# Seven quarter products for the second matrix product of eight late expert tiles, and a planner with new costs and free choice of buffers

## The chip, the cores and the metric

The kernel runs on one core of a Trainium2 chip. The metric is device time in microseconds of one execution; lower is better. All data are 32-bit floats.

## What is computed

A spectral mixing block feeds a mixture of experts.

```
X = rfft(x, axis=1); Y = X * (filt_r + i filt_i); y = irfft(Y)     x: 8 x 2496 x 256
t = y.reshape(19968, 256)
logits = t @ w_gate                                                 8 experts
e = argmax(logits); g = softmax(logits)[e]
out = g * (relu(t @ w1[e]) @ w2[e])                                 w1: 256 x 1024, w2: 1024 x 256
```

## The kernel before

**Two kinds of work.** The transform runs batch by batch in four stages of matrix products, a to d (`stage_a`, L498, to `stage_d`, L548), since 2496 = 39 x 64. Between stages the data are stored to device memory and loaded in another layout (`zd`, `ud`), except in the first batch, which stays on chip. After stage d the logits are taken, every row is given a place in the list of its expert (`route`, L707), and GpSimd scatters the rows there by indirect DMA (`scatter`, L825).

The expert work goes by tiles of rows of one expert. There are 65 in the plan: 28 of 512 rows (tiles 1 and 7 to 33), 14 of 256 rows and 23 of 128 (the last two run only if needed). `TILES`, `SHORT` and `PLACE` (L900 to 906) name them; `PLACE` is tile 34, the first 256-row tile after the last of 512 rows, and `SHORT` is 42. `rows_in` (L912) loads a tile's rows, four transfers and one for the gate values, `turn_x` (L954) transposes them on VectorE, `weights` (L933) loads a half of `w1` or `w2`, 512 KB each. The first product of the large tiles is made by seven quarter products of width 256 (`hidden_by_quarters`, L979, with sums of the weights by GpSimd in `w1_sums`, L969). The second product is made plainly (`result`, L1042): for each 128 rows eight accumulating matmuls of width 256, one instruction that scales by the gate value, one indirect DMA to the output. Until the transform has ended, and for tiles up to `PLACE`, `w2` comes in two halves per tile; from then on all of `w2` lies on chip in `w2s`, which is loaded bit by bit beside the last large tiles.

**What sets the order.** The program is straight-line code; no engine chooses. While it is built, `Order` (L125) keeps a clock for each engine and for the transfers; `count` (L177) adds an estimated time for every instruction that is issued. The main loop (L1323 to 1360) takes a transform step or a piece of expert work whose inputs are ready by these clocks: `first_products` (L1222) and `second_products` (L1259) are two streams of such pieces. `more_loads` (L1143) issues transform loads while fewer than seven input buffers are held, `prefetch` (L1186) issues rows and weights when `rows_at` (L810) says that the rows have landed. `Slots` (L243) records the buffers of a pool; a new tile takes the oldest buffer of its name in turn. PSUM has seven banks under the name `bank` (L367). SyncE issues nearly all plain DMAs, in program order, so a load waits behind whatever was issued ahead of it; GpSimd issues the indirect ones.

Nearly every instruction is recorded at L238, the line of the issuing helper, so groups are told apart by tile names: `fin` are transform inputs, `xT` the transposed rows, `hT` the hidden values, `w1t`, `w2t` the halves of the weights, `wsum` and `sums` the sums for the quarters.

Of the kernel before, what the change touches and what calls it, by code (L numbers as in the profile page):

```python
# [19 lines left out]
P = 128  # L20
# [104 lines left out]
class Order:  # L125
# [5 lines left out]
    def __init__(self, nc):  # L131
        self.nc = nc
        self.t = dict.fromkeys(("tensor", "vector", "scalar", "gpsimd", "sync", "transfers"), 0.0)
        self.slow = self.busy = self.last = 0.0
        self.done, self.used, self.slots, self.ahead = {}, {}, {}, {}
        self.tensor, self.vector, self.scalar, self.gpsimd, self.sync = (
            Issue(self, name) for name in ("tensor", "vector", "scalar", "gpsimd", "sync"))
# [33 lines left out]
    def transfer(self, out, in_):  # L171
        n = min(self.run(out), self.run(in_), 4096)
        packet = float(np.interp(n, (32, 64, 256, 1024, 4096), (9, 11, 18, 46, 159)))
        size = 4 * int(np.prod([d[1] for d in in_.ap]))
        return size / n * packet / 14e3

    def count(self, engine, op, args, named):  # L177
        aps = [a for a in list(args) + list(named.values()) if isinstance(a, bass.AP)]
        if not aps:
            return  # L180
        out, ins = aps[0], aps[1:]
        if "out" in named:
            out = named["out"]
            ins = [a for a in aps if a is not out]
        if op.endswith("value_load"):
            out, ins = None, aps
        at = named.get("out_offset")
        if at is not None:
            ins.append(at.ap)
        kept = [a for a in ins if a.space != DRAM or a.name[:2] in ("zd", "ud")]  # L190
        free = self.t[engine]
        start = max([free] + [self.ready(a) + (self.HOP if engine != "sync" else 0.0) for a in kept])
        if out is not None:
            start = max(start, self.ahead.pop(out.name, 0.0))
            n = int(np.prod([d[1] for d in out.ap][1:])) if out.space != DRAM else 0
        tail = 0.0
        if op.endswith("dma_start"):
            busy = 1.3 if engine == "gpsimd" else 0.4
            self.t[engine] = start + busy
            took = self.transfer(out, named["in_"])  # L200
            self.t["transfers"] = max(self.t["transfers"], start + busy) + took
            end, tail = self.t["transfers"], self.LOAD
        else:
            if out is None:
                took = 0.02
            elif engine == "tensor":
# [35 lines left out]

class Slots:  # L243
    def __init__(self, order, pool, bufs):
        self.order, self.pool, self.bufs, self.tiles, self.n = order, pool, bufs, {}, {}

    def free(self, tag, k=0):

        past, n = self.tiles.get(tag, []), self.n.get(tag, 0)
        if len(past) + k < n or k >= n:  # L250
            return 0.0
        name = past[k - n]
        return max(self.order.done.get(name, 0.0), self.order.used.get(name, 0.0)) + 0.1

    def tile(self, shape, dtype, **named):
        new = self.pool.tile(shape, dtype, **named)
        past = self.tiles.setdefault(named.get("tag") or named.get("name"), [])
        n = self.n[named.get("tag") or named.get("name")] = named.get("bufs") or self.bufs
        if len(past) >= n:
            name = past[-n]  # L260
            self.order.ahead[new.name] = max(self.order.done.get(name, 0.0), self.order.used.get(name, 0.0)) + 0.1
        past.append(new.name)
        return new


# [1 line left out]
def kernel(  # L267
# [86 lines left out]
    vld = cst.tile([P, 2 * NG + 2], F32, name="vld")  # L354


    first = ExitStack()
# [94 lines left out]
    ins, outs, lgs, yts, lands = {}, {}, {}, {}, []  # L452
    NIN, YB = 7, 6

    moves, stored = [], set()

# [250 lines left out]
    def route(b, c0, c1):  # L707
# [196 lines left out]
    SHORT = next(i for i in range(NT) if TILES[i][0] == 1)  # L904

    PLACE = next(i for i in range(NT) if TILES[i] == (2, B - 1))
    late = {}

    def quarters(i):
# [23 lines left out]
    def weights(h, second):  # L933
# [10 lines left out]
            return  # L944
        ev = nc.sync.value_load(work[i][1], min_val=0, max_val=E - 1)
        if second:
            w2t[h] = pools["moe"].tile([P, FH2, D], F32, tag="w2t", name="w2t", bufs=2)
            nc.sync.dma_start(out=w2t[h], in_=moe_w2[bass.ds(ev, 1), k].rearrange("o p i d -> p (o i) d"))
        else:
            pool, bufs = (late["w1"], 8) if i >= SHORT else (pools["moe"], 3)  # L950
            w1t[h] = pool.tile([P, DH, 2, 2 * P], F32, tag="w1t", name="w1t", bufs=bufs)
            nc.sync.dma_start(out=w1t[h], in_=moe_w1[bass.ds(ev, 1), k].rearrange("o p i h f -> p (o i) h f"))
# [89 lines left out]
    def result(i, j):  # L1042
# [5 lines left out]
        p = bank()  # L1048
        for k in range(FT):
            w2 = late["w2s"][:, bass.ds(ev, 1), k, :] if i >= PLACE else w2t[2 * i + k // FH2][:, k % FH2, :]  # L1050
            mm(p[:, :D], lhsT=hs[i][k % 4 // 2][:, k // 4, k % 2, j * P:(j + 1) * P], rhs=w2, start=(k == 0), stop=(k == FT - 1))
        ys = pools["moe"].tile([P, D], F32, tag="ys", name="ys", bufs=4)
        gate = gis[i][:, j, 8:9]
        either(p, D, lambda: nc.vector.tensor_scalar(ys, in0=p[:, :D], scalar1=gate, scalar2=None, op0=ALU.mult),
               lambda: nc.scalar.activation(ys, p[:, :D], AF.Copy, scale=gate))
        nc.gpsimd.indirect_dma_start(
            out=out,
            out_offset=bass.IndirectOffsetOnAxis(ap=gis[i].bitcast(U32)[:, j, :1], axis=0),
# [4 lines left out]
        )  # L1063


    sides = []

    def count(kind):
# [74 lines left out]
    def more_loads():  # L1143
# [4 lines left out]
            kind, at = {"z": ("a", zd), "u": ("c", ud)}[key[0]]  # L1148
            return (kind, key[1]) in stored and nc.ready(at[key[1]]) <= max(t["tensor"], t["sync"]) + 0.5

        while todo and len(ins) < NIN and (len(lands) < NIN or lands[-NIN] not in ins):
            n = 0
            if not stored_for(todo[0]):

# [7 lines left out]
            lands.append((kind, b, c))  # L1162

    def after(b):
        for rows, n in GROUPS[b]:
# [20 lines left out]
    def prefetch():  # L1186
# [6 lines left out]
        for what in ("w1", "w2"):  # L1193
            h = got[what]
            if h < 2 * min(len(work), NT - RARE) and rows_at[work[h // 2][3]] <= t["tensor"] and (
                    h - used[what] < ((3 if h < 2 * SHORT else 8) if what == "w1" else 2 if h < 2 * PLACE else 8)):
                weights(h, what == "w2")
                asked.add((what, h))
                got[what] += 1
        for h in range(used["w1"], got["w1"]):  # L1200
            if quarters(h // 2) and h not in wsum and len(wsum) < 2 and nc.ready(w1t[h]) <= max(t["tensor"], t["gpsimd"]) + 0.3:
                w1_sums(h)

    def when(key):

# [2 lines left out]
        if what == "w2":  # L1208
            if halves[0] <= n or key not in asked:
                return None  # L1210
            return max(ps.free("bank"), nc.ready(*hs[i], *((late["w2s"],) if i >= PLACE else (w2t[2 * i], w2t[2 * i + 1]))))
        if key not in asked or what != "x" and n % 2 and ends[0] < i:
            return None
        if what == "x":
# [44 lines left out]
    def second_products():  # L1259

        for i in range(NT - RARE):
            for j in range(TILES[i][0]):
                yield lambda: result(i, j), 3.42, ("w2", 2 * i + 1)
            hs.pop(i), gis.pop(i), w2t.pop(2 * i, None), w2t.pop(2 * i + 1, None)
            used["w2"] += 2
            ends[0] += 1

    def rare_tiles():

# [17 lines left out]
    with tc.manual_schedule(engines=None):  # L1287
# [35 lines left out]
        while fs or any(heads):  # L1323
# [27 lines left out]
            if not fs and not sides and not late:  # L1351
                fft.close()
                tail = late["tail"] = open_pool(ctx, name="tail", bufs=1)
                late["w1"] = open_pool(ctx, name="w1b", bufs=8)
                late["n"] = 0
                late["pads"] = pad_rows()
                late["w2s"] = tail.tile([P, E, FT, D], F32, name="w2s")
            prefetch()
            if used["x"] > SHORT and "need" not in late:
                late["need"] = nc.values_load(need, min_val=0, max_val=GROUPS[-1][-1][1])  # L1360
# [32 lines left out]
```

## Time and profile before

| What | Value |
|---|---|
| runs, us | 1499.45, 1493.14, 1496.27 (median 1496.27) |
| profiled execution, us | 1494.36, span 1492.7 |
| mean granted TensorE clock | 0.991 |
| TensorE busy | 1451.7 us, 7396 records |
| VectorE, ScalarE, GpSimd busy | 770.7, 471.8, 733.4 us |
| matmuls with `w2t` | 1984 records, 447.5 us busy |
| matmuls with `w2s` | 592 records, 132.6 us busy |
| VectorE adds of `hT` from a bank | 128x512: 686 ns; 128x256: 421 ns |
| GpSimd sums | 128x256: 742 ns; 128x512: 1270 ns |
| indirect DMA to the output | 161, 998 ns of GpSimd each |

A plain f32 matmul of the program is two records in the profile. The page gives busy time, count and mean length of one record for each group; records of TensorE overlap, so busy time is less than count times mean length, and the time that one takes is best read from the distance of starts in the timeline. "Idle before" is the time in which the engine stood still ahead of a group, with what ended it.

### The profile page before, as it was taken

To read this page: it belongs to the slowest core of one execution; us is meant where nothing else is said; L and a number is where in the kernel's file an instruction comes from. 1 tells how busy PE (TensorE), PEld (TensorE's weight loads), DVE (VectorE), ACT (ScalarE), POOL (GpSimd) and SP (SyncE) were. 2 spreads that over 40 slices of the span, in tenths; PEclk is the share of its full clock that TensorE was granted. 3 is DMA by queue.
4 is the path that set the end of the run, shared out by engine and by line. 5 is a ranking of instruction groups with operands and counts; after the bars stand their busy time and mean duration, and the time that the engine had idled before them with its cause. 6 is when DMAs were issued, how large, how long until landed. Compare 5 with 4: busy or idle time off the path is not lost. (4 is left out here: it accounts for less than half of the span.)

```text
span 1492.7 us, 24448 instructions
## 1 busy us (share of the span) xinstructions
PE 1451.7 (97%) x7396; PEld 1148.8 (77%) x7396; DVE 770.7 (52%) x1732; ACT 471.8 (32%) x983; POOL 733.4 (49%) x1053
## 2 busy tenths in 40 slices
PE   8898997999989999999999999999999999999998
PEld 6553555776667777777787888887888889999997
DVE  4667677354577656565764555537344334441110
ACT  4453442333322233222233222222222222223332
POOL 3434455344446656554555756764546455741111
PEclk9999999999999999999999999999999999999999
DMA  9749889678767756474456545545455543456661
GB/s 255 252 152 333 289 306 295 207 258 280 251 182 229 219 157 169 131 239 128 128 152 196 130 117 149 147 139 145 151 178 176 167 146 106 117 187 179 181 179 52
DMA packets 216376, 278.10 MB, mean 186 GB/s; under 512 B 124131, under 2 KB 163708, under 8 KB 216245
## 3 DMA queue, kind: packets, MB, share of 16 engines
q1 hardware_dynamic: 197125, 233.19, 52.7%
q0 software_dynamic: 19120, 43.33, 8.3%
q8 instruction: 62, 1.02, 0.3%
q14 instruction: 69, 0.57, 0.1%
HBM read 196.45 MB, written 80.64 MB: 186 GB/s over the span
## 5 line engine op out<-in xcount | busy, mean ns | idle before, releaser
L238 DVE TENSOR_TENSOR hT<-bank,hT 128x512 f32<-128x512 f32 (+1 forms) x504 | 300.7, 627 | 298.9 <-PE bank L238 183.1
L238 PE MATMUL bank<-w2t,hT 128*128 128x256 f32 x1984 | 447.5, 382 | 1.0 <-DVE hT L238 0.5
L238 PEld LDWEIGHTS bank<-w2t,hT 128*128 128x128 f32 x1984 | 377.6, 191 | 62.9 <-issue 9.5
L238 POOL DMA_INDIRECT out_dram<-ys,ng x161 | 160.7, 998 | 459.7 <-ACT ys L238 183.3
L238 PE MATMUL bank<-xT,w1t 128*128 128x256 f32 (+1 forms) x1728 | 316.7, 329 | 0.3 <-DVE xT L238 0.3
L238 PEld LDWEIGHTS bank<-xT,w1t 128*128 128x128 f32 x1728 | 266.8, 192 | 36.5 <-issue 11.8
L238 ACT ACTIVATE hT<-hT 128x1024 f32<-128x1024 f32 (+1 forms) x144 | 133.9, 958 | 378.7 <-DVE hT L238 374.8
L238 POOL DMA_INDIRECT rows<-yo,row x176 | 180.3, 1025 | 69.0 <-POOL yo L238 36.0
L238 ACT ACTIVATE ys<-bank,ng 128x256 f32<-128x256 f32 x128 | 60.6, 473 | 369.6 <-PE bank L238 297.0
L238 PE MATMUL bank<-sums,wsum 128*128 128x256 f32 (+1 forms) x576 | 135.7, 358 | 2.8 <-DVE hT L238 1.8
L238 PE MATMUL bank<-w2s,hT 128*128 x592 | 132.6, 380 | 0.0
L238 PEld LDWEIGHTS bank<-w2s,hT 128*128 128x128 f32 x592 | 110.5, 191 | 13.6
L238 PEld LDWEIGHTS bank<-sums,wsum 128*128 128x128 f32 x576 | 101.2, 191 | 20.1 <-issue 7.3
L238 DVE TENSOR_TENSOR ys<-bank,ht 128x512 f32<-128x512 f32 x80 | 55.0, 688 | 81.9 <-PE bank L238 77.3
L238 PE MATMUL bank<-fin,tas 117*120 117x512 f32 x154 | 76.9, 620 | 11.9 <-DMA fin<-in_x_dram 11.9
L238 PE MATMUL bank<-fin,tds 120*128 120x512 f32 (+1 forms) x168 | 76.6, 576 | 6.0 <-DMA fin<-ud 6.0
L238 DVE STREAM_TRANSPOSE xT<-xg 128x512 f32<-128x512 f32 (+2 forms) x126 | 57.5, 494 | 44.2 <-PE bank L238 44.2
L238 PE MATMUL bank<-fin,tbs 128*128 128x512 f32 x140 | 72.6, 605 | 2.5 <-DMA fin<-zd 2.5
L238 ACT ACTIVATE hT<-bank 128x128 f32<-128x128 f32 (+1 forms) x192 | 58.1, 304 | 50.1 <-PE bank L238 42.4
L238 PE MATMUL bank<-ys,tcs 128*128 128x512 f32 x140 | 72.7, 604 | 1.0 <-DVE ys L238 1.0
L238 POOL TENSOR_TENSOR wsum<-w1t 128x256 f32<-128x256 f32 x72 | 53.4, 742 | 38.1 <-PE bank L238 36.5
L238 PE MATMUL bank<-xT,wsum 128*128 128x256 f32 (+1 forms) x288 | 68.3, 360 | 0.3 <-DVE hT L238 0.3
(150 smaller groups left out, 1491.5 us busy)
## 6 DMA issues: line engine op xcount, KB each, us to landing
w1t<-in_moe_w_dram SPq DMA_DIRECT2D x126, 512.0 KB
w2t<-in_moe_w_dram SPq DMA_DIRECT2D x68, 512.0 KB
fin<-in_x_dram SPq DMA_DIRECT2D x39, 512.0 KB
fin<-zd SPq DMA_DIRECT2D x35, 512.0 KB
ud<-uo SPq DMA_DIRECT2D x35, 512.0 KB
fin<-ud SPq DMA_DIRECT2D x35, 512.0 KB
zd<-zo SPq DMA_DIRECT2D x35, 480.0 KB
xg<-rows SPq DMA_DIRECT2D x112, 128.0 KB
```

What stands on the lines that cost most here:

```text
L238: return real(*args, **named)
```

## The change

1. **Second product by quarters.** For tiles below `LARGE` (the end of the 512-row tiles) that are begun once the transform has ended, the product of 512x1024 by 1024x256 is made by seven products of a quarter each: 56 matmuls of width 128 in place of 32 of width 256. VectorE makes two sums and a difference of `hT` (`h_sums`) and one more in the loop, GpSimd three sums and a difference of `w2` (`w2_sums`), VectorE adds the products up. For this the host lays out `w2` in another way and the hidden values are indexed to match. `w2t` then has two more buffers, and four halves may be asked for ahead.
2. **Costs in the planner.** An indirect DMA costs GpSimd 1.03 in place of 1.3 us, a register load on SyncE 0.8 in place of 0.02, a transfer over at most 64 partitions with runs of 1 KB or more is 1.7 times as long, and a SyncE DMA begins only when the eighth before it has landed. Rows count as landed 3 us later.
3. **Small loads later.** `load_rest` (the tables of stage d, the gate weights and others) is put at 0.8 of the first slot of steps in place of 0.4.
4. **Any free bank or buffer.** For `bank` and the transform input buffers a new tile takes the buffer that is free first by the planner's clocks, not the oldest in turn.
5. The pool of the last tiles' `w1` is opened when the first of them is asked for, after the last 512-row tile, in the place of the quarters' pool.

```diff
-        return size / n * packet / 14e3
+        return size / n * packet / 14e3 * (1.7 if n >= 1024 and (in_ if out.space == DRAM else out).ap[0][1] <= 64 else 1.0)
...
-            busy = 1.3 if engine == "gpsimd" else 0.4
+            busy = 1.03 if engine == "gpsimd" else 0.4
+            if engine == "sync":
+                start = max(start, self.lands[-8])
...
+            if engine == "sync":
+                self.lands = self.lands[-7:] + [end + tail]
...
-                took = 0.02
+                took = 0.8 if engine == "sync" else 0.02
...
+        if tag in self.live:
+            past = self.tiles.setdefault(tag, [None] * n)
+            k = min(range(n), key=lambda k: self.freed(past[k], tag))
+            name = past[k]
+            named.update(tag=f"{tag}{k}", bufs=1)
...
+    ps.live["bank"] = lambda: ()
...
+    sb.live["in"] = lambda: {tile.name for tile in ins.values()}
...
-            rows_at[b] = nc.last
+            rows_at[b] = nc.last + 3.0
...
+    def h_sums(i):
+        a = [t.rearrange("p f v (r c) -> p r (f v) c", r=2) for t in hs[i]]
+        ss = hsum[i] = [late["quads"].tile([P, FH2, 2 * P], F32, tag="hsum", name="hsum", bufs=3) for _ in range(2)]
+        nc.vector.tensor_tensor(ss[0], a[0][:, 1], a[1][:, 1], op=ALU.add)
+        nc.vector.tensor_tensor(ss[1], ss[0], a[0][:, 0], op=ALU.subtract)
+        nc.vector.tensor_tensor(a[0][:, 1], a[0][:, 0], a[0][:, 1], op=ALU.subtract)
+
+    def w2_sums(i):
+        w = [w2t[2 * i + g].rearrange("p k (n d) -> p n k d", n=2) for g in range(2)]
+        ts = tsum[i] = late["quads"].tile([P, 3, FH2, P], F32, tag="tsum", name="tsum", bufs=2)
+        nc.gpsimd.tensor_tensor(ts[:, 0], w[0][:, 1], w[0][:, 0], op=ALU.subtract)
+        nc.gpsimd.tensor_tensor(ts[:, 1], w[1][:, 1], ts[:, 0], op=ALU.subtract)
+        nc.gpsimd.tensor_tensor(ts[:, 2], w[1][:, 0], ts[:, 1], op=ALU.subtract)
+        nc.gpsimd.tensor_tensor(w[0][:, 1], w[1][:, 1], w[0][:, 1], op=ALU.subtract)
+
+    def result_by_quarters(i):
...
+        def product(left, right):
+            q = bank()[:, :D].rearrange("p (j d) -> p j d", j=2)
+            for j in range(2):
+                for k in range(FH2):
+                    mm(q[:, j], lhsT=left[:, k, j * P:(j + 1) * P], rhs=right[:, k], start=k == 0, stop=k == FH2 - 1)
+            return q
...
+        q = product(a[0][:, 0], w[0][:, 0])
+        nc.scalar.copy(out=one, in_=q)
+        q = product(a[1][:, 0], w[1][:, 0])
+        add(top[:, :, 0], q, one)
+        q = product(ss[1], ts[:, 1])
+        add(two, q, one)
+        nc.vector.tensor_tensor(a[1][:, 0], a[1][:, 0], ss[1], op=ALU.subtract)
+        q = product(a[0][:, 1], w[0][:, 1])
+        add(three, q, two)
+        q = product(ss[0], ts[:, 0])
+        add(low[:, :, 1], q, three)
+        add(four, q, two)
+        q = product(a[1][:, 1], ts[:, 2])
+        add(low[:, :, 0], q, three)
+        q = product(a[1][:, 0], w[1][:, 1])
+        add(top[:, :, 1], q, four)
...
-            steps.append((0.4, load_rest, None, 0.0, None))
+            steps.append((0.8, load_rest, None, 0.0, None))
...
-        while todo and len(ins) < NIN and (len(lands) < NIN or lands[-NIN] not in ins):
+        while todo and len(ins) < NIN and sb.free("in") <= max(t["tensor"], t["sync"]) + 0.5:
...
-                late["w1"] = open_pool(ctx, name="w1b", bufs=8)
...
+                late["quads"] = open_pool(quads, name="quads", bufs=1)
...
-        moe_w2=inputs["moe_w2"].reshape(E, 2, FT // 2, P, D).transpose(0, 1, 3, 2, 4),
+        moe_w2=inputs["moe_w2"].reshape(E, 2, 2, 2, P, D).transpose(0, 2, 4, 1, 3, 5).reshape(E, 2, P, FT // 2, D),
```

More of the change, by code (lines that the diff above doesn't have):

```diff
@@ L134, in __init__ @@
         self.slow = self.busy = self.last = 0.0
+        self.lands = [0.0] * 8
         self.done, self.used, self.slots, self.ahead = {}, {}, {}, {}
@@ L244, in __init__, with freed @@
     def __init__(self, order, pool, bufs):
-        self.order, self.pool, self.bufs, self.tiles, self.n = order, pool, bufs, {}, {}
+        self.order, self.pool, self.bufs, self.tiles, self.n, self.live = order, pool, bufs, {}, {}, {}
+    def freed(self, name, tag):
+        if name is None:
+            return 0.0
+        if tag in self.live and name in self.live[tag]():
+            return 1e9
+        return max(self.order.done.get(name, 0.0), self.order.used.get(name, 0.0)) + 0.1
     def free(self, tag, k=0):
         past, n = self.tiles.get(tag, []), self.n.get(tag, 0)
+        if tag in self.live:
+            return sorted(self.freed(name, tag) for name in past)[k] if past else 0.0
         if len(past) + k < n or k >= n:
             return 0.0
-        name = past[k - n]
-        return max(self.order.done.get(name, 0.0), self.order.used.get(name, 0.0)) + 0.1
+        return self.freed(past[k - n], tag)
     def tile(self, shape, dtype, **named):
-        new = self.pool.tile(shape, dtype, **named)
[L257 to L262, printed above, removed]
+        tag = named.get("tag") or named.get("name")
+        n = self.n[tag] = named.get("bufs") or self.bufs
+        if tag in self.live:
+            past = self.tiles.setdefault(tag, [None] * n)
+            k = min(range(n), key=lambda k: self.freed(past[k], tag))
+            name = past[k]
+            named.update(tag=f"{tag}{k}", bufs=1)
+        else:
+            past = self.tiles.setdefault(tag, [])
+            name = past[-n] if len(past) >= n else None
+        new = self.pool.tile(shape, dtype, **named)
+        if name is not None:
+            self.order.ahead[new.name] = self.freed(name, None)
+        if tag in self.live:
+            past[k] = new.name
+        else:
+            past.append(new.name)
         return new
@@ L354 @@
     vld = cst.tile([P, 2 * NG + 2], F32, name="vld")
-    first = ExitStack()
+    first, quads = ExitStack(), ExitStack()
     pro = open_pool(first, name="pro", bufs=2, side="right")
@@ L450, in columns @@
             yield NS, slice(m, n), rows[(NG - 1) * TK:, :].rearrange("(i p) d -> p i d", p=NS)
-    ins, outs, lgs, yts, lands = {}, {}, {}, {}, []
+    ins, outs, lgs, yts = {}, {}, {}, {}
     NIN, YB = 7, 6
+    sb.live["in"] = lambda: {tile.name for tile in ins.values()}
     moves, stored = [], set()
@@ L906 @@
     PLACE = next(i for i in range(NT) if TILES[i] == (2, B - 1))
+    LARGE = 1 + max(i for i in range(NT) if TILES[i][0] == 4)
     late = {}
@@ L946, in weights @@
         if second:
-            w2t[h] = pools["moe"].tile([P, FH2, D], F32, tag="w2t", name="w2t", bufs=2)
+            w2t[h] = (late["quads"] if late and late["flip"] else pools["moe"]).tile([P, FH2, D], F32, tag="w2t", name="w2t", bufs=2)
+            if late and k:
+                late["flip"] = not late["flip"]
             nc.sync.dma_start(out=w2t[h], in_=moe_w2[bass.ds(ev, 1), k].rearrange("o p i d -> p (o i) d"))
         else:
+            if i >= SHORT and "w1" not in late:
+                late["w1"] = open_pool(ctx, name="w1b", bufs=8)
             pool, bufs = (late["w1"], 8) if i >= SHORT else (pools["moe"], 3)
@@ L1050, in result @@
             w2 = late["w2s"][:, bass.ds(ev, 1), k, :] if i >= PLACE else w2t[2 * i + k // FH2][:, k % FH2, :]
-            mm(p[:, :D], lhsT=hs[i][k % 4 // 2][:, k // 4, k % 2, j * P:(j + 1) * P], rhs=w2, start=(k == 0), stop=(k == FT - 1))
+            mm(p[:, :D], lhsT=hs[i][k // FH2][:, k % FH2 // 2, k % 2, j * P:(j + 1) * P], rhs=w2, start=(k == 0), stop=(k == FT - 1))
         ys = pools["moe"].tile([P, D], F32, tag="ys", name="ys", bufs=4)
@@ L1055, in result, with deliver @@
                lambda: nc.scalar.activation(ys, p[:, :D], AF.Copy, scale=gate))
+        deliver(i, j, ys)
+    def deliver(i, j, ys):
         nc.gpsimd.indirect_dma_start(
@@ L1063, in result @@
         )
+    hsum, tsum, needs = {}, {}, {}
+    def h_sums(i):
[4 more added lines that the diff above has]
+        nc.vector.tensor_tensor(a[0][:, 1], a[0][:, 0], a[0][:, 1], op=ALU.subtract)
@@ new lines, in result_by_quarters, with part, add, send @@
+    def result_by_quarters(i):
+        a = [t.rearrange("p f v (r c) -> p r (f v) c", r=2) for t in hs[i]]
+        w = [w2t[2 * i + g].rearrange("p k (n d) -> p n k d", n=2) for g in range(2)]
+        gate = gis[i][:, :, 8:9]
+        def product(left, right):
[4 more added lines that the diff above has]
+            return q
+        def part(name):
+            return late["quads"].tile([P, 2, P], F32, tag=name, name=name, bufs=1)
+        def add(o, q, b):
+            nc.vector.tensor_tensor(o, q, b, op=ALU.add)
+        def send(j, y):
+            ys = pools["moe"].tile([P, D], F32, tag="ys", name="ys", bufs=4)
+            nc.scalar.activation(ys, y.rearrange("p n d -> p (n d)"), AF.Copy, scale=gate[:, j])
+            deliver(i, j, ys)
+        one, two, three, four = (part(name) for name in ("one", "two", "three", "four"))
+        top, low = (late["quads"].tile([P, 2, 2, P], F32, tag=name, name=name, bufs=1) for name in ("top", "low"))
+        q = product(a[0][:, 0], w[0][:, 0])
+        nc.scalar.copy(out=one, in_=q)
+        needs[i] = [hs[i][1]]
+        yield
+        q = product(a[1][:, 0], w[1][:, 0])
+        add(top[:, :, 0], q, one)
+        needs[i] = None
+        yield
+        ss, ts = hsum[i], tsum[i]
+        q = product(ss[1], ts[:, 1])
+        add(two, q, one)
+        nc.vector.tensor_tensor(a[1][:, 0], a[1][:, 0], ss[1], op=ALU.subtract)
+        needs[i] = []
+        yield
+        q = product(a[0][:, 1], w[0][:, 1])
+        add(three, q, two)
+        yield
+        q = product(ss[0], ts[:, 0])
+        add(low[:, :, 1], q, three)
+        add(four, q, two)
+        yield
+        q = product(a[1][:, 1], ts[:, 2])
+        add(low[:, :, 0], q, three)
+        for j in range(2):
+            send(2 + j, low[:, j])
+        needs[i] = [hs[i][1]]
+        yield
+        q = product(a[1][:, 0], w[1][:, 1])
+        add(top[:, :, 1], q, four)
+        for j in range(2):
+            send(j, top[:, j])
+        hsum.pop(i), tsum.pop(i), needs.pop(i)
+        yield
@@ L1160, in more_loads @@
             {"x": load_x, "z": load_z, "u": load_u}[kind](b, c)
-            lands.append((kind, b, c))
     def after(b):
@@ L1195, in prefetch @@
             if h < 2 * min(len(work), NT - RARE) and rows_at[work[h // 2][3]] <= t["tensor"] and (
-                    h - used[what] < ((3 if h < 2 * SHORT else 8) if what == "w1" else 2 if h < 2 * PLACE else 8)):
+                    h - used[what] < ((3 if h < 2 * SHORT else 8) if what == "w1" else (4 if late and h < 2 * LARGE else 2) if h < 2 * PLACE else 8)
+                    and (what == "w2" or h < 2 * SHORT or ends[0] >= LARGE)):
                 weights(h, what == "w2")
@@ L1202, in prefetch @@
                 w1_sums(h)
+        i = used["w2"] // 2
+        if late and i < LARGE and halves[0] > 2 * i + 1 and i not in hsum and ends[0] == i and i in wide and nc.ready(*hs[i]) <= max(t["tensor"], t["vector"]) + 0.3:
+            h_sums(i)
+        for i in (used["w2"] // 2, used["w2"] // 2 + 1):
+            if late and i < LARGE and (i in wide or i > used["w2"] // 2) and i not in tsum and len(tsum) < 2 and 2 * i + 1 in w2t and nc.ready(w2t[2 * i], w2t[2 * i + 1]) <= max(t["tensor"], t["gpsimd"]) + 0.3:
+                w2_sums(i)
+    wide = set()
     def when(key):
@@ L1211, in when @@
             return max(ps.free("bank"), nc.ready(*hs[i], *((late["w2s"],) if i >= PLACE else (w2t[2 * i], w2t[2 * i + 1]))))
+        if what == "wide":
+            if halves[0] <= n or ("w2", n) not in asked:
+                return None
+            more = needs.get(i, [hs[i][0], w2t[2 * i]])
+            if more is None:
+                if i not in hsum or i not in tsum:
+                    return None
+                more = [*hsum[i], tsum[i]]
+            return max(ps.free("bank"), nc.ready(*more))
         if key not in asked or what != "x" and n % 2 and ends[0] < i:
@@ L1261, in second_products, with go @@
         for i in range(NT - RARE):
-            for j in range(TILES[i][0]):
-                yield lambda: result(i, j), 3.42, ("w2", 2 * i + 1)
+            if late and i < LARGE:
+                wide.add(i)
+                steps = None
+                for j in range(7):
+                    def go():
+                        nonlocal steps
+                        steps = steps or result_by_quarters(i)
+                        next(steps)
+                    yield go, 1.79, ("wide", 2 * i + 1)
+            else:
+                for j in range(TILES[i][0]):
+                    yield lambda: result(i, j), 3.42, ("w2", 2 * i + 1)
             hs.pop(i), gis.pop(i), w2t.pop(2 * i, None), w2t.pop(2 * i + 1, None)
@@ L1266, in second_products @@
             ends[0] += 1
+            if ends[0] == LARGE:
+                quads.close()
     def rare_tiles():
@@ L1357 @@
                 late["w2s"] = tail.tile([P, E, FT, D], F32, name="w2s")
+                late["flip"] = True
+                late["quads"] = open_pool(quads, name="quads", bufs=1)
             prefetch()
```

## The prediction

> **What bounds the kernel now.** I read the page's busy shares first, then its slices, then busy time per stretch, then TensorE's timeline where it had holes. The chain of waits is of no use here: it covers only the last 12 us.
>
> ```profile
> span 1492.7 us, 24448 instructions
> PE 1451.7 (97%) x7396; PEld 1148.8 (77%) x7396; DVE 770.7 (52%) x1732; ACT 471.8 (32%) x983; POOL 733.4 (49%) x1053
> PE   8898997999989999999999999999999999999998
> DMA  9749889678767756474456545545455543456661
> ```
>
> TensorE is busy for 97% of the span. The missing 41.0 us lie in the first slices and in a few single holes; from about 1040 us to the tail there is none. DMA is near its full share only in the first 250 us. So there are two separate prices: TensorE work (each us saved is a us of time) and the holes of the transform stage.
>
> The late stage has pure blocks of both matmul widths. Rows of the timeline: start, length, engine, operation, count.
>
> ```profile
> 1381.44 3.74 PE L238 MATMUL bank<-xT,w1t 128*128 128x128 f32 x32
> 1385.01 3.62 PE L238 MATMUL bank<-w2s,hT 128*128 x16
> 1388.47 3.73 PE L238 MATMUL bank<-xT,w1t 128*128 128x128 f32 x32
> ```
>
> The reader should use the starts, not the lengths, which overlap. 32 records of width 128 take 1385.01 - 1381.44 = 3.57 us, 0.1116 each. 16 records of width 256 take 3.46 us, 0.2163 each. A matmul in f32 is two records, so 0.223 us at width 128 and 0.433 at width 256: half the width costs 52%, not 50%.
>
> The holes that the diff's planner changes could reach, in TensorE's timeline:
>
> ```profile
> 134.95 3.75 PE L238 MATMUL bank<-fin,tds 120*128 120x512 f32 x4 [5.96 <-DMA fin<-ud]
> ...
> 243.94 3.74 PE L238 MATMUL bank<-fin,tas 117*120 117x512 f32 x4 [6.92 <-DMA fin<-in_x_dram]
> 247.47 2.48 PE L238 MATMUL bank<-xT,w1t 128*128 128x256 f32 x8
> ...
> 431.76 0.65 PE L238 MATMUL lt<-yt,wb 128*32 128x128 f32 x16 [3.08 <-DVE yt L238]
> ```
>
> The one at 237 to 244 us is explained by SyncE's queue:
>
> ```profile
> 230.85 1.89 SPq L238 DMA_DIRECT2D xg<-rows  x4
> 232.93 0.40 SPq L238 DMA_DIRECT2D ng<-rows  x1
> 234.13 0.36 SPq L238 DMA_DIRECT2D w1t<-in_moe_w_dram  x1
> 235.29 0.34 SPq L238 DMA_DIRECT2D w2t<-in_moe_w_dram  x1
> 236.04 0.38 SPq L238 DMA_DIRECT2D fin<-ud  x1
> 236.53 0.44 SPq L238 DMA_DIRECT2D fin<-in_x_dram  x1
> ```
>
> The x load that TensorE wants at 237.0 is issued at 236.53, behind two whole expert tiles (each five row loads and two weight loads, some 5.5 us of SyncE from 225.1 to 230.85 to 236.0). The planner charged 0.02 us for each register load between them.
>
> **What the Trainium skill says.** "TensorE: Matmul & The Clock Gate", Part 1: after an idle window of about 3.4 us the array runs at half rate until it has been busy again. The trace agrees: after the 6.92 us hole the four fin,tas records take 3.53 us from start to start where four took 1.72 at 108.86, and the eight after them 2.32 against 1.73, so this hole costs 6.92 + 1.8 + 0.6 = 9.3 us. The same page, Back-to-back issue gap, gives a small constant per matmul on top of width over clock; the 52% above agrees in kind. "SBUF — State Buffer", Who interferes with whom: a DVE instruction with two SBUF inputs and a GpSimd one that reads SBUF exclude each other for a whole instruction. The trace agrees: ys<-ys,yw (both inputs in SBUF) took 1.26 us at 240.08, beside GpSimd sums, and 0.69 at 243.38.
>
> **The change, part by part.**
>
> 1. *Second product by quarters.* In the instruction lists of the two programs 256 matmuls of width 256 are gone and 448 of width 128 have come: eight tiles (26 to 33), 32 against 56 each. Removed: 64 x 0.2163 = 13.84 us a tile. Added: 112 x 0.1116 = 12.50. Saved: 1.34 a tile, 10.7 us in eight, all on TensorE, which has no hole there.
>
> 2. *Sums that the quarters need.* DVE: four of 128x1024 a tile, SBUF to SBUF. Not shown before; from hT<-bank,hT, 421 ns at 256 columns and 686 at 512, that is 265 ns per 256 columns: estimate 1.22 us each, 4.9 us; up to 1.3 more each if a GpSimd sum (1.27 at 128x512) holds the port. Seven combinations at 421 ns: 2.9 us. DVE is busy 39% in 1100 to 1250 us, so about 10.1 of 25.9 us a tile; it gets to 17.9 of 24.6, or 23 with every collision. GpSimd: four of 128x512, 1.27 each (row ys<-ys,yw x16), 5.1 us; it goes from 55% (14.3) to about 19.4 of 24.6. ACT: one copy more (362 ns). What hides them is 14 first-product matmuls of width 256 per half tile (6.05 us) and the other quarter products. Where DVE's queue is longest: after the second half of a tile ends come its last add and the relu (2.4 us), then three sums (3.7, with collisions 5.6): DVE is free at 6.1 to 8.0. In the instruction order TensorE meanwhile has one quarter product, eight matmuls, a second quarter product and four more, 1.8 + 3.5 + 1.8 + 1.7 = 8.8 us, before the first product that needs the sums, and fills at most seven banks on the way. Behind the sums in DVE's queue wait the bank adds of the next tile; with seven banks they may be 7 us late. I take 0 for stalls; bounds 0 and 1.3 a tile (one collision, all of it showing), so 0 to +10.
>
> 3. *w2 layout and four half tiles of w2 ahead.* The same loads, 512 KB each; DMA is at about half share there. 0.
>
> 4. *Order: SyncE register loads cost 0.8, rows planned 3 us later, at most eight SyncE DMAs in flight.* In the new list the fin,tas pair that stood before the 512-row tile's first product comes after 28 matmuls of that tile and more: at least 12 us of TensorE work now stand where the hole was. That removes 9.3 us. Moved with it: the row loads (five DMAs a tile), their weights and the loads behind them on SyncE; GpSimd's scatters that the rows wait for are not moved past. What comes late next is that very tile: its wsum was done at 237.3 in the trace, its transposes at 231.6, so it could have started where the hole began; 3 us later still costs up to 3.
>
> 5. *Small loads later.* tds, wg, wb, ids, vld (eight DMAs, SyncE from 30.68 to 38.9 us) move behind an x load and two stores. Here DMA is full and the next x load still stands behind the fourth store (issued by 39.9), so it can start no earlier than 40; the load after it now stands behind the small ones. Gain of the first against loss of the second: I take 0, bounds -3 and +3.
>
> 6. *Any free bank or buffer.* No large wait of TensorE on a bank is in the list of waits: 0. For buffers: within part 7.
>
> 7. *Everything else that the new order shuffles between 100 and 1020 us.* The hole at 129 to 135 us (a u load in a full DMA) has the same neighbours in the new list: about 15.8 us of work from the end of stage c to the first fin,tds against 14.7 before. The DVE run of small tile-map operations that made the holes at 428 us (about 7 us with the slow clock) and 1012 us is still there; at 1012 it is instruction for instruction the same, at 428 its neighbours differ. Work that fills a DMA-bound stretch (the first eight xT,w1t matmuls, near 160 us) is put nine 512-column matmuls, about 8 us, later. I charge +4 us for a new hole, half of one like those shown; bounds -9 (one more hole gone) and +10 (one new hole of the kind above).
>
> Sum: -10.7 + 0 + 0 - 9.3 + 0 + 4 = -16.0. The profiled execution took 1494.36 (span 1492.7 and 1.7 around it), so its like would take 1478.4. The median of the runs is 1.9 higher, 1496.27, which gives 1480.
>
> **Rivals.**
> - *The order gives back what it gains* (the hole moves instead of going): only the quarters remain, with small stalls, 1496.3 - 10.7 + 0 to 8 = 1486 to 1494. For it: DMA is full from 100 to 250 us, and the holes there are a matter of bytes, not of order. Against: 12 us of ready work now cover the x load.
> - *The quarters save nothing*: reading busy over count for width 128 (105.3 us over 864) gives 0.122, and 112 x 0.122 = 13.7, as before. Against: pure blocks show 0.1116. Then 1496.3 - 9.3 + 4 = 1491.
> - *A further hole goes*: 1480 - 10 = 1470. For it: more work before the u loads of batches 2 and 3 (23 against 11 us in batch 2).
> - *Slower*: the rows planned later leave TensorE without expert work in the DMA-bound stretch from 100 to 250 us. Each load it then waits for costs 6 to 7 us and 2.4 of slow clock, about 9. The old hole in another place and two more: 1496.3 - 10.7 + 18 = 1504. It decides from the point where two such holes outweigh the quarters. For it: DMA at full share there. Against: the first expert tiles are few in both orders.
>
> **How the numbers follow.** About 0.5% (7.5 us) is what a measurement can tell from no change: below 1488.8 is faster, above 1503.8 slower. Forecast, around 1480: 0.47. The order gives back its gain: 0.25, of which about 0.14 below 1488.8. No saving by quarters: 0.08, within. A further hole: 0.13. Slower: 0.07, of which 0.05 past the bound. Faster 0.47 + 0.14 + 0.13 = 0.74, same 0.21, slower 0.05. Range: down to the further hole with its own bound, 1467; up to the upper end of the given-back case and its spread (the runs differ by 6 us), 1496.
>
> **What would show it.** Right: quarter products in blocks of 0.1116 a record, PE without holes from 1040 us on, 448 matmuls of width 128 in place of 256; no wait near 237 us for in_x; PE busy near 1441. Wrong: TensorE waits for hsum, tsum or wsum in the late stage (part 2); new waits for fin<-zd or fin<-ud over 3 us between 100 and 300 us (part 7); a PE clock below 0.99.

## The result and the profile after

The changed kernel takes 1531.26 us (median of six runs, 1526.76 to 1537.19), the kernel before beside it 1497.76 (six runs, 1493.14 to 1499.45): ratio 1.0231, 95% interval 1.0209 to 1.0253. It is slower by some 34 us where 1480 was forecast. The profiled execution took 1534.2 us with a span of 1532.5, at a mean granted clock of 0.982 (0.991 before).

The page after, in the rows that were shown of before:

```profile
span 1532.5 us, 25409 instructions
PE 1461.2 (95%) x7780; PEld 1160.2 (76%) x7780; DVE 837.1 (55%) x1811; ACT 476.9 (31%) x1000; POOL 793.5 (52%) x1085
PE   8798998999999999999999999999988888999998
DMA  9649898786875776556456444456543423456661
```

The span grew by 39.8 us. TensorE's busy time grew by 9.5 in spite of the shorter products, its idle time by 30.3. The slices tell where: 30 to 34 of 40 (1111 to 1303 us), full before, show eights. GpSimd's busy share warns of nothing, 52% of the span. One row of the page does, that of the matmuls with `wsum`, which had 2.8 us of idle time ahead of them before:

```profile
L243 PE MATMUL bank<-sums,wsum 128*128 128x256 f32 (+1 forms) x576 | 140.2, 367 | 26.3 <-POOL wsum L243 26.3
```

TensorE's timeline of that stretch:

```profile
1144.32 1.95 PE L243 MATMUL bank<-tsum,hsum 128*128 128x128 f32 x16
1146.11 1.95 PE L243 MATMUL bank<-tsum,hT 128*128 128x128 f32 x16
1147.89 1.95 PE L243 MATMUL bank<-w2t,hT 128*128 128x128 f32 x16
...
1163.89 1.61 PE L243 MATMUL bank<-sums,wsum 128*128 128x256 f32 x4 [4.49 <-POOL wsum L243]
1165.29 1.91 PE L243 MATMUL bank<-xT,w1t 128*128 128x256 f32 x4
```

The quarters are as forecast: 16 records of width 128 start 1.78 or 1.79 us apart, 0.1116 each. But a product of the next tile's second half waits 4.49 us for `wsum`, and its four records take 1.40 us from start to start (1165.29 - 1163.89) where 0.87 is usual: the clock fell too. From 1040 us on TensorE waits for `wsum` 12 times, 26.3 us in all, and 2.9 us for the `w1t` that the same sums change.

GpSimd's timeline tells why `wsum` is late:

```profile
1101.65 0.99 POOL L243 DMA_INDIRECT out_dram<-ys,ng  x1 [0.15 <-issue]
1104.86 0.98 POOL L243 DMA_INDIRECT out_dram<-ys,ng  x1 [2.21 <-DMA out_dram<-ys,ng]
1110.90 0.98 POOL L243 DMA_INDIRECT out_dram<-ys,ng  x1 [5.07 <-DMA out_dram<-ys,ng]
1116.85 0.98 POOL L243 DMA_INDIRECT out_dram<-ys,ng  x1 [4.97 <-DMA out_dram<-ys,ng]
1117.85 0.74 POOL L243 TENSOR_TENSOR wsum<-w1t 128x256 f32<-128x256 f32 x1
```

The four output scatters of a tile stand one behind the other, and each waits in the queue until the one before has landed, that is, until its rows have been written. GpSimd does nothing meanwhile. `wsum` is made twice a tile, once right behind the scatters and once behind the sums of `w2`. TensorE waits for either: 3.40 us at 1119.45 for the first, 4.49 at 1163.89 for the second, begun at 1160.47. In the kernel before the scatters come as the results come, 3.45 us apart, and `wsum` has time to spare, as GpSimd's timeline of before shows:

```profile
1207.79 0.99 POOL L238 DMA_INDIRECT out_dram<-ys,ng  x1 [0.42 <-ACT ys L238]
1211.24 0.98 POOL L238 DMA_INDIRECT out_dram<-ys,ng  x1 [2.46 <-ACT ys L238]
1214.70 0.98 POOL L238 DMA_INDIRECT out_dram<-ys,ng  x1 [2.48 <-ACT ys L238]
1219.99 0.73 POOL L238 TENSOR_TENSOR wsum<-w1t 128x256 f32<-128x256 f32 x1 [4.32 <-PE bank L238]
```

There GpSimd waits 4.32 us for TensorE: it is ahead. In these tiles of the changed kernel its sums never wait for TensorE. Its rounds, from the `wsum` after one tile's scatters to that after the next, begin at 1084.85, 1117.85, 1148.48, 1178.30, 1206.46 and 1236.10: 30.25 us on average, against 24.6 that TensorE needs for a tile (the forecast's figure; experiment 3 has it too, 1086.98 to 1111.57). The round from 1117.85 adds up so: `wsum` 2.9, `sums` 2.9, the four sums of `w2` 5.2, the second `wsum` 5.7 (three of its four sums took 1.6 to 1.7 us), scatters 14.0, of which 10.1 are waits. The round is full without being busy.

The "DMA: Bandwidth & Descriptors" page of the Trainium skill, section Anatomy of one DMA, SWDGE path, gives a DMA from GpSimd about 2.0 us of fixed time, most of it the receipt of the last write, plus its bytes over 436 GB/s; for 128 KB that makes an estimate of 2.3. The usual short wait here, 2.21 us, agrees; 5.07 and 4.97 do not. SyncE's queue shows what stood beside these two, loads of weights of 512 KB each:

```profile
1104.65 0.35 SPq L243 DMA_DIRECT2D w1t<-in_moe_w_dram  x1
1105.04 0.43 SPq L243 DMA_DIRECT2D w2s<-in_moe_w_dram  x1
1108.99 0.33 SPq L243 DMA_DIRECT2D w2t<-in_moe_w_dram  x1
1109.37 0.44 SPq L243 DMA_DIRECT2D w2s<-in_moe_w_dram  x1
```

In the five rounds every one of the five waits over 4 us follows a scatter that was issued within 2 us after such a load; none of the ten waits of 2.2 to 2.4 us does. The two go together in the trace; no experiment held the loads away from the scatters.

In the transform stage the hole at 237 us is gone and others stand in its place, by TensorE's timeline of after:

```profile
60.57 3.74 PE L243 MATMUL bank<-fin,tas 117*120 117x512 f32 x4 [6.10 <-DMA fin<-in_x_dram]
...
146.62 5.68 PE L243 MATMUL bank<-fin,tds 120*128 120x512 f32 x8 [3.36 <-DMA fin<-ud]
...
253.93 2.07 PE L243 MATMUL bank<-ys,tcs 128*128 128x512 f32 x2 [3.52 <-DVE yw L243]
```

### The profile page after: what moved, and what is told of

Read it like the earlier page. It is cut to its first block, busy times and chain, and to the rows that moved or that the text cites. A ratio compares the mean times of both kernels' runs of the same rounds, so it can differ in the third digit from the quotient of the medians.

```text
span 1532.5 us, 25409 instructions
## 1 busy us (share of the span) xinstructions
PE 1461.2 (95%) x7780; PEld 1160.2 (76%) x7780; DVE 837.1 (55%) x1811; ACT 476.9 (31%) x1000; POOL 793.5 (52%) x1085
## 5 line engine op out<-in xcount | busy, mean ns | idle before, releaser
L243 PE MATMUL bank<-w2t,hT 128*128 128x256 f32 (+1 forms) x1984 | 398.2, 356 | 3.4 <-DVE hT L243 3.4
L243 PEld LDWEIGHTS bank<-w2t,hT 128*128 128x128 f32 x1984 | 343.2, 193 | 54.5 <-issue 10.5
L243 PE MATMUL bank<-xT,w1t 128*128 128x256 f32 (+1 forms) x1728 | 320.5, 332 | 2.9 <-POOL w1t L243 2.9
L243 PE MATMUL bank<-sums,wsum 128*128 128x256 f32 (+1 forms) x576 | 140.2, 367 | 26.3 <-POOL wsum L243 26.3
L243 PEld LDWEIGHTS bank<-sums,wsum 128*128 128x128 f32 x576 | 101.9, 195 | 50.1 <-POOL wsum L243 30.2
L243 ACT ACTIVATE ys<-bank,ng 128x256 f32<-128x256 f32 x97 | 46.0, 474 | 298.0 <-PE bank L243 261.1
L243 PEld LDWEIGHTS bank<-w2s,hT 128*128 128x128 f32 x592 | 110.3, 190 | 13.8
L243 POOL TENSOR_TENSOR wsum<-w1t 128x256 f32<-128x256 f32 x72 | 57.7, 801 | 21.9 <-PE bank L243 18.9
```

Of the source, the lines that this page charges most:

```text
L243: return real(*args, **named)
```

## The experiments

Theory: dependent scatters in a row hold GpSimd's queue, and `wsum` and so TensorE are late. Rivals: GpSimd's sums collide with VectorE's on the port of SBUF (the on-chip memory) that the prediction names; the new order is to blame.

**1. The quarters alone.** Everything in the planner is put back, the quarters stay:

```diff
-                took = 0.8 if engine == "sync" else 0.02
+                took = 0.02
-            rows_at[b] = nc.last + 3.0
+            rows_at[b] = nc.last
-            steps.append((0.8, load_rest, None, 0.0, None))
+            steps.append((0.4, load_rest, None, 0.0, None))
-    ps.live["bank"] = lambda: ()
...
```

> The quarters with the order of before: every cost and choice of the planner is put back, only the second product by quarters is left. Queue theory (each output scatter waits on GpSimd for the one before it to land, four close together hold GpSimd, and wsum behind them is late for TensorE): all of the loss of the late stage stays, 1497.8 + 27 = about 1525, with TensorE waiting over 20 us for wsum. Port theory (the new SBUF sums of VectorE and GpSimd exclude each other and make GpSimd late): the same 1525, so this run does not part the two. Order theory (the loss comes from the new order): about 1487.

Measured: 1529.83 us, ratio 1.0227 (1.0197 to 1.0258), the same `wsum` waits (30.7 us of TensorE from 1040 us on). The loss comes with the quarters.

**2. The order alone.** The new planner, no quarters:

```diff
-            if late and i < LARGE:
+            if False and late and i < LARGE:
                 wide.add(i)
...
```

> The new order with the plain second product, no sums for it. Queue and port theory: the late stage is as before, and only what the new order costs in the transform stage is left, 0 to +8, so 1498 to 1506; a hole of about 6 us near 60 us and none at 237 us. Order theory: 1531.

Measured: 1494.56 us, ratio 1.0003 (0.9986 to 1.0019). The order costs nothing that can be measured (-2.1 to +2.8 us), and does not bring its forecast 5 us. The hole at 237 us is gone here too, but TensorE waits 6.11 us for an x load at 56.47 and 3.51 for VectorE's `yw` at 247.36.

**3. The scatters freed.** They write rows of their own, so they need not wait for one another. The changed kernel with only this:

```diff
-        nc.gpsimd.indirect_dma_start(
+        sc = nc.gpsimd.indirect_dma_start(
             out=out,
...
         )
+        tc.declare_no_dep(sc.ins, group="output", reason="rows of their own")
+        tc.add_to_no_dep_group("output", sc.ins)
```

> The changed kernel with the output scatters declared independent of each other (they write different rows), nothing else moved. Queue theory: no waits of 2 to 5 us of GpSimd for an earlier output scatter, TensorE's waits for wsum fall from 26 us to under 5, the quarters give their 10.7: 1531 - 38 - 0 to 5 = 1488 to 1494. Port theory: the sums still collide, 1.6 to 1.7 us in place of 0.73 on GpSimd, and the time stays over 1520.

Measured: 1481.35 us, ratio 0.9908 (0.9879 to 0.9936). GpSimd's timeline:

```profile
1103.45 0.99 POOL L243 DMA_INDIRECT out_dram<-ys,ng  x1 [0.25 <-ACT ys L243]
1104.74 0.98 POOL L243 DMA_INDIRECT out_dram<-ys,ng  x1 [0.30 <-issue]
1106.03 0.98 POOL L243 DMA_INDIRECT out_dram<-ys,ng  x1 [0.30 <-issue]
1107.31 0.98 POOL L243 DMA_INDIRECT out_dram<-ys,ng  x1 [0.30 <-issue]
1110.04 0.72 POOL L243 TENSOR_TENSOR wsum<-w1t 128x256 f32<-128x256 f32 x1 [1.75 <-PE bank L243]
```

Four scatters in 4.8 us instead of 16.2, and GpSimd waits for TensorE again. From 1040 us on TensorE's longest wait is 0.2 us. With the same matmuls it is busy for 1443.2 us instead of 1461.2, at a granted clock of 0.992 instead of 0.982: of the 51.5 us of span 18.0 go with the slower clock, the other 33.5 were idle.

**4. The quarters alone, scatters freed** (the edits of 1 and 3):

> The quarters in the order of before, with independent output scatters. Queue theory: 1497.8 - 10.7 = 1487, with up to 4 us less gain for collisions on the port. Port theory: about 1520.

Measured: 1487.27 us, ratio 0.9949 (0.993 to 0.9967). This is the forecast's first term together with whatever the sums still cost: 0.0051 of 1496 is 7.6 us, interval 4.9 to 10.5, for 10.7.

**5. Control: the kernel before, scatters freed** (the edit of 3):

> The kernel before with only this changed: its output scatters no longer wait for one another. Queue theory (a scatter waits in GpSimd's queue for the one before to land, and that costs only where scatters come close together): in the kernel before they come one result, 3.46 us, apart and the wait hides, so no change: 1493 to 1498. Rival (the wait costs in any order, and freeing it is a gain of its own that the changed kernel only shares): 8 us or more faster, under 1489.

Measured: 1495.71 us, ratio 1.0002 (0.9992 to 1.0012). The wait was there all along and cost nothing.

**6. The scatters spread.** They still wait for one another, but the changed kernel issues one at a time, after each quarter product:

```diff
-            deliver(i, j, ys)
+            later.append((i, gis[i], j, ys))
...
                         next(steps)
+                        one_later()
```

> The changed kernel with its scatters still waiting for one another, but issued one per quarter product (about 3.4 us of TensorE work apart) instead of four in a row. Queue theory: the wait hides again as in the kernel before and most of the 50 us comes back: 1481 to 1497, and no wait of TensorE for wsum over 2 us. Rival (GpSimd has too much to do with the sums of w2, in whatever order): most of the loss stays, 1515 to 1531.

Measured: 1500.81 us, ratio 1.004 (1.0016 to 1.0063). From 1040 us on the longest wait for `wsum` is 1.02 us, and three fifths of the 50 us are back. It just misses the range, and is slower than with free scatters by more than the profile shows (its profiled execution, 1492.38, is the lowest of its runs, which reach 1506.07); where the rest goes stays open.

**7. Free scatters, small loads early:** the edit of 3, and `load_rest` at 0.4 again.

> The changed kernel with free scatters (1481.35 measured) and the small loads put back where the kernel before had them. If the small loads are what the x load before the hole at 57 to 60 us stands behind, the hole of 6.1 us shrinks: 1473 to 1478. Rival (the same bytes have to pass DMA in any order, the hole only moves): 1479 to 1484.

Measured: 1479.19 us, ratio 0.9883 (0.985 to 0.9916), at the lower edge of the rival's range and not told apart from 1481.35. TensorE's timeline shows the hole as an exchange:

```profile
60.78 2.04 PE L243 MATMUL bank<-fin,tbs 128*128 128x512 f32 x2 [3.38 <-DMA fin<-zd]
...
142.43 6.82 PE L243 MATMUL bank<-fin,tds 120*128 120x512 f32 x8 [5.07 <-DMA fin<-ud]
```

The x load, which in experiment 3 holds TensorE for 6.52 us at 59.99, no longer does; a store and load of `zd` holds it for 3.38. And the later hole, 3.36 us in the changed kernel, is 5.07 here. In experiment 3, whose program has the transform of the changed kernel, that later hole is missing, so part of this can be chance of one execution.

**8. The kernel before with its scatters in a row.** No quarters; the four scatters of a late 512-row tile below tile 29 are held back until its last result:

```diff
+        outq.append((gis[i], j, ys))
+        if not late or TILES[i][0] != 4 or i >= 29 or j == 3:
+            while outq:
+                g, jj, yy = outq.pop(0)
+                nc.gpsimd.indirect_dma_start(
...
```

> The kernel before with one change: in the late stage, up to the 29th tile, the four output scatters of a 512-row tile (four or five such tiles) are held back until its last result and then issued in a row, waiting for one another as before. No quarters, no sums of w2. Queue theory: wsum stands behind them and TensorE waits 3 to 5 us for it at each bunch, with some slow clock after: 1510 to 1530, with rows that name POOL wsum. Rival (it takes the quarters' own work to make wsum late): no change, 1493 to 1499.

Measured: 1496.41 us, ratio 1.0 (0.9989 to 1.0012). The theory missed. GpSimd waited for its scatters 24.9 us between 1085 and 1165 (22.1 in the changed kernel), and TensorE felt nothing: GpSimd, with 46.9 us busy, was held for 71.8 of 80 us and kept up. A queue of waiting scatters is not enough; the waits have to fill the time that GpSimd's work leaves.

**9. The changed kernel without GpSimd's sums of `w2`** (the products take `w2`'s own quarters, and the result is not the reference's):

```diff
-        ss, ts = hsum[i], tsum[i]
-        q = product(ss[1], ts[:, 1])
+        ss, ts = hsum[i], (w[0][:, 1], w[1][:, 1], w[1][:, 0])
+        q = product(ss[1], ts[1])
...
```

> The changed kernel, its four scatters in a row still waiting for one another, with GpSimd's four sums of w2 left out: the quarter products take w2's own quarters instead, so the second product's values are not those of the reference. The theory as the last runs leave it (GpSimd is the bound when its busy time and its waits for its own scatters together fill a tile's time; it takes the scatters in a row and the sums): GpSimd is held for about 72 of 80 us between 1085 and 1165, and TensorE no longer waits for wsum: 1481 to 1497. Rival (the scatters in a row are enough, wherever the sums are): 1515 to 1531.

Measured: 1491.07 us, ratio 0.9972 (0.9956 to 0.9989): the time is as the theory had it, with the scatters in a row all the same. Between 1085 and 1165, first by the table of stretches (length, then busy time and count of PE, PEld, DVE, ACT and POOL, clock, DMA share, GB/s), then by the list of GpSimd's waits:

```profile
1085.00:1165.00 80.00, 80.00 (x547) 75.25 (x546) 59.52 (x89) 24.37 (x37) 42.81 (x49) 1.00 0.56 169
```

```profile
POOL out_dram L243 <- DMA out_dram<-ys,ng: 35.5, 10, 4.4
```

TensorE is busy all through, and from 1040 us on it waits for `wsum` for 3.4 us in all, 1.02 at the longest. GpSimd is held for 42.8 + 35.5 = 78.3 us, not for the 72 expected: it fills the time to the brim and no more. Seven of the ten waits are of 3.6 to 4.4 us, each after a scatter issued within 0.6 us of a weight load; the three others are of 2.2 to 2.5, with no such load near.

**10. The kernel before, scatters in a row, and four sums of `w2` that nobody reads** (the edit of 8, and):

```diff
...
+            for k in range(4):
+                nc.gpsimd.tensor_tensor(ts[:, k], w[k // 2][:, 1 - k % 2], w[1 - k // 2][:, 0], op=ALU.subtract)
```

> The kernel before with the scatters of four or five late tiles issued in a row (1496.41 measured, no loss) and with GpSimd also making four sums of w2 for each of those tiles (128x512, into a scratch tile that nobody reads). No quarter products, nothing more on VectorE. GpSimd full by work and waits together: 71.8 of 80 us held before, 16 to 22 more now is over 80, so TensorE waits for wsum in those tiles: 1503 to 1515. Rival (the loss needs VectorE's sums or the quarters' order too): 1494 to 1500.

Measured: 1499.63 us, ratio 1.0017 (1.0004 to 1.003), so 0.6 to 4.5 us and not 7 to 19; the time lies in the rival's range. The trace shows the mechanism all the same: GpSimd's rounds begin at 1048.23, 1078.51, 1108.21 and 1138.94, 30.2 us each, while TensorE takes 25.9 a tile. What the expectation left out is the lead. The `wsum` of 1048.23 is wanted at 1064.79, that of 1138.94 at 1142.49; the lead shrinks by over 4 us a tile, and TensorE waits only after the last of these tiles. That more of them would have cost more follows from these rounds, but was not tried:

```profile
1149.72 1.13 PE L238 MATMUL bank<-sums,wsum 128*128 128x256 f32 x4 [1.02 <-POOL wsum L238]
```

**11. Free scatters, small loads early, rows not planned later** (7, and `rows_at[b] = nc.last`):

> The changed kernel with free scatters, the small loads early (1479.19 measured) and the rows no longer planned 3 us later. If the later rows are what removed the hole at 237 us, it comes back: 1484 to 1490. If the register loads' cost of 0.8 and the limit of eight loads removed it, no change: 1477 to 1482. If the later rows made the new hole at 250 us (VectorE yw), it goes: 1473 to 1477.

Measured: 1479.37 us, ratio 0.9872 (0.984 to 0.9905), as 7. TensorE's timeline:

```profile
141.64 6.78 PE L243 MATMUL bank<-fin,tds 120*128 120x512 f32 x8 [3.98 <-DMA fin<-ud]
235.80 1.26 PE L243 MATMUL bank<-fin,tbs 128*128 128x512 f32 x2 [2.76 <-DMA fin<-zd]
```

The wait for `yw` at 250 us, 3.5 us in the traces of the changed kernel and of experiments 2, 3, 6 and 7, is gone, so the later rows had brought it; the old hole of 6.92 us does not return, so not the later rows but the planner's other costs, or its free choice of buffers, had removed it. In its place stands a wait of 2.76 us for `zd`. The sum is unchanged.

**12. The changed kernel without VectorE's sums of `h`** (the products take `h`'s own quarters, and the result is not the reference's):

```diff
-        ss, ts = hsum[i], tsum[i]
+        ss, ts = (a[0][:, 1], a[1][:, 1]), tsum[i]
-        nc.vector.tensor_tensor(a[1][:, 0], a[1][:, 0], ss[1], op=ALU.subtract)
...
```

> The changed kernel, scatters in a row and waiting, GpSimd's sums of w2 kept, with VectorE's four sums of h left out: the quarter products take h's own quarters, so the second product's values are not those of the reference. It weighs the port: in the changed kernel GpSimd's round of a tile took 30.25 us (five rounds between 1084.85 and 1236.10), about 10 of it waits for its scatters, 5.2 sums of w2 and some 3 sums that ran at 1.6 to 1.7 us beside VectorE's instead of 0.73. Theory (the round is a sum, all three count): without VectorE's sums a round of 27 to 28 us, against 24.6 of TensorE: 1503 to 1517. Rival 1 (the port adds nothing to the loss): 1525 to 1531. Rival 2 (the port is what tips it): under 1497.

Measured: 1508.17 us, ratio 1.011 (1.0088 to 1.0132), in the range of the theory; both rivals fall. In the profiled execution the rounds that begin at 1078.96, 1103.91, 1130.24, 1155.30, 1180.36 and 1206.64 take 25.5 us on average, shorter than the 27 to 28 expected (that execution, 1501.15, is the lowest of its runs, which reach 1512.03). GpSimd's 128x256 sums of weights take 725 to 735 ns on average there, 860 to 1071 in the changed kernel. One row of each list of GpSimd's groups between 1040 and 1260 us, here and in the changed kernel:

```profile
L243 POOL TENSOR_TENSOR wsum<-wsum,w1t 128x256 f32<-128x256 f32 x18 | 13.1, 725 | 1.4
L243 POOL TENSOR_TENSOR wsum<-wsum,w1t 128x256 f32<-128x256 f32 x15 | 16.1, 1071 | 1.2
```

The shorter sums are not all of it: of the 4.7 us by which a round is shorter, 1.7 are shorter waits for the scatters (7.8 a round for 9.5).

## Why the prediction was wrong

The step that failed is part 2, "I take 0 for stalls; bounds 0 and 1.3 a tile ... so 0 to +10". By experiment 3 against the result it cost 0.0323 of 1496, 48 us. The dependent output scatters hold GpSimd's queue, and the sums of `w2` take the room that this leaves. The sums themselves stall nothing: with the scatters freed no wait of TensorE over 0.2 us is left in the late stage, and the changed kernel takes 1481.35, one microsecond from the forecast. That nearness is partly luck: 0.9908 is -13.8 us (-18.1 to -9.6) for -16.0, and the terms differ from their forecasts by more than the sum.

- *Part 1, quarters, -10.7.* Right in kind, rather large: experiment 4 gives -7.6 (-10.5 to -4.9).
- *Part 2, sums.* "It goes from 55% (14.3) to about 19.4 of 24.6" was a sum of busy times. It was nearly right as such: without the waits a round is 20.8 us (30.25 less 47.4 us of waits in five rounds, 9.5 each). The queue's waits were missing. The list of waits of before had them, this row of GpSimd's being among its longest:

```profile
POOL out_dram L238 <- DMA out_dram<-ys,ng: 65.0, 22, 6.8
```

  They cost nothing there (experiment 5): results came 3.45 us apart, and where scatters stood in a row GpSimd had room for the waits (experiment 8). The quarters deliver two pairs close together, and all four scatters stand in a row ahead of `wsum`, in the order of before too (experiment 1). The edit that moved the scatters was costed for VectorE, GpSimd's sums and the banks, not for these DMAs, so this wait was never priced. The price was at hand: the trace of before has 2.21 us for the scatter of 1056.73 behind the one before it, and three such waits a tile come to 6.6, and 19.4 + 6.6 = 26.0 is already over 24.6.
- *The port.* The forecast counted collisions for VectorE. They came: VectorE's sums took 1.26 to 1.74 us on average by group for an estimated 1.22, and GpSimd's 128x256 sums 1.6 to 1.7 for 0.73, as "SBUF — State Buffer", Who interferes with whom, has it. In experiment 3 they are there and cost nothing. In the full round they count: without VectorE's sums the loss over the free kernel falls from about 48 us to 30 (1.011 against 0.9908), of which the shorter waits of experiment 12 are a part.
- *Parts 4, 5 and 7, order, -5.3 net.* With free scatters the order is worth 0.9908 against 0.9949, some 6 us (1 to 11); alone (experiment 2) at most 2. A gain of 1 to 2 us would fit both. The named hole went, as part 4 said, but what came late next was not the expert tile: it was VectorE's `yw`, 3.5 us and six records at half rate (3.57 us from 253.93 on, where 1.73 is usual), brought by the rows planned later (experiment 11). For part 5 I took 0, and experiment 7 against 3 shows no difference: a hole at 57 to 60 us against one at 137 to 142.
- *The rivals.* None named GpSimd's queue. The slower rival, 1504, put its holes in the DMA-bound stretch; the loss came in the late stage, where DMA has room. The signs that the prediction set for "wrong" did appear: waits for `wsum`, a clock below 0.99, and a wait of 3.36 us for `fin<-ud`.

What is settled: it takes the scatters' waits and the sums of `w2` together, and VectorE's sums make it worse (12). Free the scatters (3) or leave out the sums of `w2` (9) and no wait for `wsum` over 1.02 us is left; in the kernel before, the scatters in a row alone (8) cost nothing, and with sums (10) GpSimd falls back by over 4 us a tile, though over so few tiles that costs little time. What is open: whether the long landings come from the weight loads beside them, as the traces suggest, and what experiment 6 still pays.

The fastest version is the changed kernel with free scatters and the small loads early (7), 1.2% faster than the kernel before; 11 is its equal.

## What to carry to other kernels

Cost an in-order queue by its time held, busy plus the waits at its head, against the time that the consumer allows, and count the DMAs that an edit bunches together: a dependent scatter costs its landing, not its issue. A wait that hides in the kernel before hides by a distance between instructions or by room in its queue; before moving or adding any, ask how much of each there is. And a queue that is too slow shows only after its lead is used up: in a short trial compare the lengths of rounds, not stalls.

## What the runs showed of the hardware

A scatter of 128 rows of 1 KB holds GpSimd for 0.98 us and releases the next dependent one about 2.2 us after its record at the soonest. Waits of 4 to 6.6 us are common (6.59 in experiment 10): in the five rounds of the changed kernel each follows a scatter issued within 2 us after a 512 KB weight load, and none of the short waits does. Free scatters follow each other at 1.29 us. GpSimd's sums of 128x256 took 0.73 us, and 1.6 to 1.7 beside VectorE's sums of 128x1024.

With holes of 1 to 4.5 us and little work between them TensorE's mean clock was 0.96 between 1040 and 1300 us; over the whole execution its busy time was 18.0 us longer than with free scatters. "TensorE: Matmul & The Clock Gate", Part 1, speaks of idle windows of about 3.4 us. Here four records after holes of 2.95 and 0.54 us, close together, took 1.86 us from start to start (1133.85 to 1135.71) where 0.87 is usual; after 2.28 and 0.54 they took 0.97 (1194.37 to 1195.34).
